# The second expert product of the last two groups as seven block products instead of eight

## The chip, the cores and the metric

The kernel runs on one core of a Trainium2 chip. The metric is the device time of one execution in microseconds (us); lower is better. Before the change the median of three runs is 1410.24 us (1410.23 to 1412.16). One further execution was profiled, and all views below come from it. The engines are named as the profile names them: PE (TensorE, matrix products; PEld is its weight load), DVE (VectorE), ACT (ScalarE), POOL (GpSimd), SP (the engine that issues the DMAs here).

## The reference

An attention over 32 memory slots feeds a mixture of four dense experts that are all computed and weighted:

```
a = softmax(phi, over s)                     # per batch b and head h
k_m, v_m = a^T k, a^T v                      # 32 x 64 each
attn = softmax(q k_m^T / 8)                  # 576 x 32
x = (attn v_m), heads side by side           # 4608 x 512
p = domain_probs / sum(domain_probs)
for e in range(4):
    h = max(x @ w1[e], 0)                    # 4608 x 1024
    out += p[:, e] * (h @ w2[e])             # 4608 x 512
```

Shapes: 8 batches, 8 heads, 576 rows per batch, 512 model columns, 1024 hidden columns, fp32.

## The kernel before

**Numbers.** Every operand of a large product is kept as two fp32r tiles, high part and rest. A product is three matmuls that add up in PSUM: high x high, high x rest, rest x high. The high part is made by an ACT copy (or relu), the rest by a subtraction on DVE or POOL. w1 is multiplied into v_m first (the tiles `vw`), so the first product of an expert is `vw` against the attention weights `AT`.

**Stages.** The rows go in four groups k of two batches (1152 rows, nine tiles of 128). A group takes PAIR = 128 steps: 4 experts x 2 batches (`odd`) x 2 halves of a batch x NJ = 8 blocks j of 128 hidden columns. A batch of 576 rows is cut into 256 + 320 or 320 + 256 rows (`HALF`), so that the 64 rows left over of both batches make the ninth tile (`mid`, name hm).

**One step.** `first(s + 2)` issues six matmuls (lines 553 to 555, two sets of three) of 256 or 320 columns into PSUM, ACT makes relu's high part (line 565), DVE the rest (line 567), into `h` and, for the 64 rows, into `hm`. `second(s)` then multiplies h of two steps ago by w2: three matmuls of 512 columns for each of two row tiles (lines 583 to 585), and three more for hm in the third of four passes. The sum over j stays in PSUM (`p2`, four banks) for eight steps; at the end of a pass `accumulate` lets DVE multiply it by the expert's probability and add it to `acc` in SBUF (lines 603, 605), which goes out after the fourth expert (line 607).

**Other work, by a table of steps.** `plan[s]` holds what is issued ahead of the matmuls of step s. Attention of the later batches stands at the steps of `ATT`. Weights arrive by `take` through four staging tiles (`stage`, line 133) and are split by `split` (ACT line 147, POOL or DVE line 148). For groups 2 and 3 `four` computes the products of w1 and v_m for four batches at once, and writes them to device memory (`vst`, lines 506 to 509, store at 492); `load_vw` (line 531) reads them back. In group 2 this stands in 16 of the 32 steps of each of the first three experts (steps 8 to 23, splits from step 6), one `four` a step. w2 of the next expert is loaded and split at steps 29 to 36 of each expert (`units_w2`), in every group.

**Order.** From step 36 on every engine runs its instructions in the order in which the code issues them (`manual_schedule`); all DMAs are issued by SP, in one queue.

## Time and profile before

| | |
|---|---|
| median of three runs | 1410.24 us |
| profiled execution, span from first to last instruction | 1409.6 us |
| instructions in the span | 21662 |
| first expert of group 2 begins (first matmul of its step 0) | 766.8 us |
| first expert of group 3 begins | 1101.4 us |
| bytes moved by DMA | 200.47 MB, mean 142 GB/s |

The profiled execution gives no time of its own but its span; it is 0.6 us under the median of the runs. In a row of matmuls the time from one start to the next is what PE spends; the duration printed is longer, since matmuls overlap. In a row of a group the columns are: line, engine, operation, tile written and tiles read, shapes, count, then busy us and mean ns of one, then idle time ahead of it and who ended it.

### The profile page before, as it was taken

The page shows a single profiled execution, that of the slowest core. Times are in us where ns is not written, and L with a number is a line of the kernel's source. Part 1 is how long each engine was busy: PE and PEld are TensorE (multiplying, and loading weights), DVE is VectorE, ACT ScalarE, POOL GpSimd, SP SyncE. Part 2 cuts the span into 40 slices and gives each one's busy share as a digit, 9 for nine tenths or more (in the row PEclk, how much of TensorE's full clock was granted, in tenths as well). Part 3 has the DMA queues.
Part 4 walks back from the last instruction along what each step waited for, and adds up shares of the span by engine and source line. Part 5 has one row for each costly group of instructions (what it writes and reads, how often), then busy time and mean ns, then how long its engine had stood idle before and what let it go on. Part 6 is the DMA issues. An engine that isn't in the chain of part 4 may idle for free.

```text
span 1409.6 us, 21662 instructions
## 1 busy us (share of the span) xinstructions
PE 1391.7 (99%) x7742; PEld 1217.9 (86%) x7742; DVE 624.5 (44%) x1470; ACT 579.6 (41%) x1536; POOL 400.7 (28%) x324
## 2 busy tenths in 40 slices
PE   7999999999999999999999999999999999999998
PEld 6888888888888888888888888888888888888887
DVE  7875535435553465344353445434343223222232
ACT  6755555433354456553353434435322312122221
POOL 4400354422234244441342424434220202020200
PEclk9999999999999999999999999999999999999999
DMA  6532332684232243333588675776742623233201
GB/s 251 184 96 75 123 98 91 231 253 128 76 130 95 71 143 109 111 98 105 138 299 243 234 257 173 277 216 224 240 123 64 176 67 105 76 105 76 60 31 38
DMA packets 74363, 200.47 MB, mean 142 GB/s; under 512 B 21904, under 2 KB 23056, under 8 KB 74256
## 3 DMA queue, kind: packets, MB, share of 16 engines
q1 hardware_dynamic: 74256, 199.09, 44.9%
q8 instruction: 62, 1.02, 0.3%
q14 instruction: 45, 0.37, 0.1%
HBM read 146.35 MB, written 51.38 MB: 140 GB/s over the span
## 4 chain that ended last, share of the span: by engine, by line
PE 93%; ACT 2%; DVE 2%; DMA 1%; issue 1%; SPq 0%; ACTq 0%
PE p L585 18%; PE p L583 18%; PE p L584 18%; PE p L553 10%; PE p L554 9%; PE p L555 9%; PE pv L506 3%; PE sc L391 2%; PE x L287 2%; PE pv L461 1%; PE pv L463 1%; PE pv L462 1%; DVE vw L482 1%; DMA stage<-in_w 1%; PE tp L441 1%
## 5 line engine op out<-in xcount | busy, mean ns | idle before, releaser
L148 POOL TENSOR_TENSOR w<-stage,w 128x512 fp32r<-128x512 f32 x230 | 297.2, 1293 | 719.4 <-ACT w L147 698.3
L567 DVE SCALAR_TENSOR_TENSOR h<-p,h 128x256 fp32r<-128x256 f32 x512 | 215.6, 421 | 443.3 <-ACT h L565 300.6
L585 PE MATMUL p<-w,h 128*128 128x512 f32 x1024 | 402.4, 393 | 0.9 <-DVE h L567 0.9
L583 PE MATMUL p<-w,h 128*128 128x512 f32 x1024 | 403.0, 394 | 0.0
L584 PE MATMUL p<-w,h 128*128 128x512 f32 x1024 | 402.3, 393 | 0.0
L565 ACT ACTIVATE h<-p 128x256 fp32r<-128x256 f32 x512 | 196.4, 384 | 484.8 <-PE p L555 465.5
L553 PE MATMUL p<-AT,vw 128*128 128x256 f32 (+1 forms) x1024 | 308.9, 302 | 2.3 <-DVE h L567 0.9
L554 PE MATMUL p<-AT,vw 128*128 128x256 f32 (+1 forms) x1024 | 302.7, 296 | 0.0
L555 PE MATMUL p<-AT,vw 128*128 128x256 f32 (+1 forms) x1024 | 301.5, 295 | 0.0
L585 PEld LDWEIGHTS p<-w,h 128*128 128x128 f32 x1024 | 192.5, 188 | 44.8 <-DVE h L567 1.4
L553 PEld LDWEIGHTS p<-AT,vw 128*128 128x128 f32 x1024 | 193.2, 189 | 22.6 <-DVE h L567 1.2
L583 PEld LDWEIGHTS p<-w,h 128*128 128x128 f32 x1024 | 192.4, 188 | 22.9
L584 PEld LDWEIGHTS p<-w,h 128*128 128x128 f32 x1024 | 192.5, 188 | 21.8
L554 PEld LDWEIGHTS p<-AT,vw 128*128 128x128 f32 x1024 | 193.8, 189 | 19.6
L555 PEld LDWEIGHTS p<-AT,vw 128*128 128x128 f32 x1024 | 192.8, 188 | 0.1
L147 ACT CAST w<-stage 128x512 fp32r<-128x512 f32 x264 | 161.9, 618 | 6.8 <-DMA stage<-in_w 4.6
L567 DVE SCALAR_TENSOR_TENSOR hm<-p,hm 128x64 fp32r<-128x64 f32 x256 | 56.1, 219 | 156.8 <-ACT h L565 155.7
L565 ACT ACTIVATE hm<-p 128x64 fp32r<-128x64 f32 x256 | 57.1, 223 | 161.5 <-PE p L555 161.5
L509 DVE TENSOR_TENSOR vst<-pv,vst 128x512 fp32r<-128x512 f32 x80 | 55.3, 692 | 113.2 <-ACT vst L508 112.9
L276 POOL TENSOR_TENSOR kvs<-stage,kvs 128x512 fp32r<-128x512 f32 x58 | 75.8, 1326 | 103.9 <-ACT kvs L275 103.5
L508 ACT CAST vst<-pv 128x512 fp32r<-128x512 f32 x80 | 46.9, 587 | 123.6 <-PE pv L506 123.6
L482 DVE TENSOR_TENSOR vw<-pv,vw 64x512 fp32r<-64x512 f32 x96 | 65.9, 688 | 24.7 <-ACT vw L480 23.5
(87 smaller groups left out, 1147.4 us busy)
## 6 DMA issues: line engine op xcount, KB each, us to landing
stage<-in_w SPq DMA_DIRECT2D x92, 512.0 KB, 4.2
vwd<-vst SPq DMA_DIRECT2D x80, 512.0 KB, 3.6
vw<-vwd SPq DMA_DIRECT2D x320, 128.0 KB, 3.8
stage<-in_w1d SPq DMA_DIRECT2D x40, 512.0 KB, 3.9
stage<-in_kv SPq DMA_DIRECT2D x32, 512.0 KB, 4.1
stage<-in_qm SPq DMA_DIRECT2D x16, 512.0 KB, 3.9
out<-acc SPq DMA_DIRECT2D x32, 256.0 KB, 2.1
ph<-in_phi SPq DMA_DIRECT2D x16, 288.0 KB, 4.4
```

The source lines that it names most:

```text
L147: nc.scalar.copy(dst[:, 0, :], raw)
L148: eng.tensor_sub(dst[:, 1, :], raw, dst[:, 0, :].bitcast(F32))
L276: eng.tensor_sub(t[:, 1], src, t[:, 0].bitcast(F32))
L482: nc.vector.tensor_sub(t[r, 1, :], ps[r], t[r, 0, :].bitcast(F32))
L553: nc.tensor.matmul(ps, w[:, 0, f], at_t[:, g, 0, c], start=g == 0, stop=False)
L554: nc.tensor.matmul(ps, w[:, 0, f], at_t[:, g, 1, c], start=False, stop=False)
L555: nc.tensor.matmul(ps, w[:, 1, f], at_t[:, g, 0, c], start=False, stop=g == 1)
L565: nc.scalar.activation(t[:, 0, to], ps[:, at_], AF.Relu)
L567: nc.vector.scalar_tensor_tensor(t[:, 1, to], ps[:, at_], 0.0, t[:, 0, to].bitcast(F32), ALU.max, ALU.subtract)
L583: nc.tensor.matmul(po[t], x[:, 0, :], w[:, 0, :], start=j == 0, stop=False)
L584: nc.tensor.matmul(po[t], x[:, 0, :], w[:, 1, :], start=False, stop=False)
L585: nc.tensor.matmul(po[t], x[:, 1, :], w[:, 0, :], start=False, stop=j == NJ - 1)
```

## The change

For groups 2 and 3 (`SEVEN = 2`), `first` and `second` are replaced by 64 units. A unit is 256 rows (two tiles of 128) against 512 hidden columns (four blocks j) and all 512 columns of w2: the work of four steps. It is a 2 x 2 block product (row tiles x halves of the hidden columns, times halves of the hidden columns x halves of the output columns). It is computed from seven block products in place of eight, by Winograd's form of Strassen's scheme: the left sides are A11, A12, A22 and four sums t1, t2, t3, n4 of blocks, the right sides blocks of w2 and four sums of them. Each product is six matmuls of 256 columns. The first product of the experts (`rows`, now lines 854 to 856) and the 64 left-over rows (`middle`) are computed as before.

- Left sums are made by DVE straight from PSUM with the relu (`x_out`, `y_diff`, `y_last`), then split by ACT and POOL.
- Products add up in two PSUM banks in turn; some partial sums are added to `acc` for one output block, and then the next product is accumulated on top. So DVE adds seven times 256 columns per unit (`add_in`) in place of two times 512 columns per eight steps.
- The sums of w2 (`sums`, eight jobs in groups 0 and 1 by the table `JOBS`) are made by POOL, split, and kept in device memory, as is the split w2 of group 1 (`leave`, `leave_now`). `units_w2` is gone for groups 2 and 3: a block of four units reads eight tiles of 512 KB back into a ring of eleven (`load_part`, `free`).
- PSUM is one tile of eight banks with turns kept by hand. In the units banks 2 to 5 hold the first product and 6 and 7 the seven products; two banks are left for the other work.
- The reading back of `vw` for groups 2 and 3 stands at other steps (`VW_LOAD_7`), and so do the last transposes of batch 7.

```diff
-    7: (PAIR + 62, PAIR + 88, (2 * PAIR + 98, 2 * PAIR + 102, 2 * PAIR + 106), (2 * PAIR + 112, 2 * PAIR + 113, 2 * PAIR + 114)),
+    7: (PAIR + 62, PAIR + 88, (2 * PAIR + 98, 2 * PAIR + 102, 2 * PAIR + 106), (2 * PAIR + 115, 2 * PAIR + 116, 2 * PAIR + 117)),
...
+SEVEN = 2
+BEGIN = SEVEN * PAIR
+UNITS = (NG - SEVEN) * E * 2 * 4
+Q = 256
+X_BANK, Y_BANK, AB_BANK = 4, 2, 6
+JOBS = (92, 101, 110, 119, 127, PAIR + 23, PAIR + 62, PAIR + 86)
+VW_LOAD_7 = ((18, 32), (24, 40))
+FIRST_LOADS = (PAIR + 112, PAIR + 121, PAIR + 122, PAIR + 123, PAIR + 124, PAIR + 125, PAIR + 126, PAIR + 127)
 
...
-    psum = pool("psum", space=PSUM)
+    banks = pool("psum", space=PSUM).tile([P, 8, 512], F32, name="banks")
+    turns = {"pm": [0, 0, 4], "p2": [0, 4, 4]}
...
+        if k == SEVEN - 1:
+            leave(("w2", e, j), t)
...
+    def leave_now():
+        for key, t in leaving:
+            kept_for[key] = dram.tile([P, 2, DM], F32, name="k" + "".join(map(str, key)))
+            nc.sync.dma_start(kept_for[key], t.bitcast(F32))
+        leaving.clear()
+    def sums(s, e, fh):
+        kept = []
+        top, low = slice(0, Q), slice(Q, DM)
+        sub, g = nc.gpsimd.tensor_sub, nc.gpsimd
+        at(s, (("w2", e, 2 * fh), kept.append))
+        at(s + 1, (("w2", e, 2 * fh + 1), kept.append))
+        at(s + 1, lambda: g.tensor_add(kept[1][:, :, low], kept[0][:, :, low], kept[1][:, :, low]))
+        at(s + 2, lambda: sub(kept[0][:, :, low], kept[0][:, :, top], kept[0][:, :, low]))
+        at(s + 2, lambda: sub(kept[0][:, :, top], kept[1][:, :, low], kept[0][:, :, top]))
+        at(s + 3, lambda: sub(kept[1][:, :, top], kept[1][:, :, top], kept[0][:, :, top]))
+        def out(i):
+            t = att.tile([P, 2, DM], F32R, name="sv", tag="kvs", bufs=KVS)
+            split(t, kept[i // 2][:, i % 2, :], g)
+            leave(("v", e, fh, i), t)
+        for i in range(4):
+            at(s + 3 + i, lambda i=i: out(i))
+            at(s + 4 + i, leave_now)
...
-        if s >= LAST:
+        if s >= BEGIN:
...
-            for j2 in range(4):
+            for j2 in range(4 if nk < SEVEN else 0):
                 for i, u in enumerate(units_w2(nk, ne, j2)):
                     at(s + W2_FROM + 2 * j2 + i, u)
+                    if nk == SEVEN - 1:
+                        at(s + W2_FROM + 2 * j2 + i + 1, leave_now)
...
-                    at(s + VW_LOAD_AT[odd][fh], lambda a=(nk, ne, odd, fh): load_vw(*a))
+                    when = VW_LOAD_AT if nk < SEVEN else VW_LOAD_7
+                    at(s + when[odd][fh], lambda a=(nk, ne, odd, fh): load_vw(*a))
...
+    for n, s in enumerate(JOBS):
+        sums(s, n // 2, n % 2)
+    for s in FIRST_LOADS:
+        at(s, lambda: load_part(wp.tile([P, 2, DM], F32R, name="w2", tag="w2", bufs=NJ + 1)))
...
+    def free(u, *which):
+        if u % 4 == 3:
+            for i in which:
+                ring.extend(W[u // 4][i, jj] for jj in range(2))
...
+    def open_ring():
+        ring.append(wp.tile([P, 2, DM], F32R, name="w2", tag="w2", bufs=NJ + 1))
+        ring.append(att.tile([P, 2, 512], F32R, name="vw", tag="vw1", bufs=5))
+        ring.append(wp.tile([P, 2, 512], F32R, name="w1", tag="w1", bufs=4))
...
+    def x_out(u):
+        if u >= UNITS:
+            return
+        g = ph2["g"]
+        a = work.tile([P, 2, 2, P], F32R, name="a1", tag="h", bufs=AHEAD + 2)
+        t = work.tile([P, 2, 2, P], F32R, name="t1", tag="h", bufs=AHEAD + 2)
+        VE.scalar_tensor_tensor(g[:, 2], ps_of(u, 0)[:, 1], 0.0, g[:, 0], ALU.max, ALU.subtract)
+        AC.copy(a[:, 0], g[:, 0])
+        GP.tensor_sub(a[:, 1], g[:, 0], a[:, 0].bitcast(F32))
+        mids(u, 0)
+        AC.copy(t[:, 0], g[:, 2])
+        GP.tensor_sub(t[:, 1], g[:, 2], t[:, 0].bitcast(F32))
+        op["a11", u], op["t1", u] = a, t
+    def y_hi(u):
+        if u < UNITS:
+            AC.activation(ph2["Y"][u % 2][:, 0], flat_of(u, 1), AF.Relu)
+    def y_diff(u):
+        if u < UNITS:
+            src, g, d = ps_of(u, 1)[:, 1], ph2["g"], ph2["d"]
+            for i in range(2):
+                VE.scalar_tensor_tensor(d[:, i], src, 0.0, g[:, 1 + i], ALU.max, ALU.subtract)
+    def y_lo(u):
+        if u >= UNITS:
+            return
+        y, d, D = ph2["Y"][u % 2], ph2["d"], ph2["D"][u % 2]
+        VE.scalar_tensor_tensor(y[:, 1], flat_of(u, 1), 0.0, y[:, 0].bitcast(F32), ALU.max, ALU.subtract)
+        op["a12", u], op["a22", u] = y[:, :, :, :P], y[:, :, :, P:]
+        AC.copy(D[:, 0], d)
+        GP.tensor_sub(D[:, 1], d, D[:, 0].bitcast(F32))
+        op["t3", u], op["t2", u] = D[:, :, 0], D[:, :, 1]
+    def y_last(u):
+        if u >= UNITS:
+            return
+        n, N4 = ph2["n"], ph2["N"][u % 2]
+        VE.scalar_tensor_tensor(n, ps_of(u, 1)[:, 0], 0.0, ph2["d"][:, 1], ALU.max, ALU.subtract)
+        mids(u, 1)
+        AC.copy(N4[:, 0], n)
+        GP.tensor_sub(N4[:, 1], n, N4[:, 0].bitcast(F32))
+        op["n4", u] = N4
...
+    def product(u, name, place, side, b, start, stop):
+        a, ps = op[name, u], banks[:, AB_BANK + (u + b) % 2, :Q]
+        c = slice(Q * side, Q * side + Q)
+        for jj in range(2):
+            w = W[u // 4][place, jj]
+            for i, (l, r) in enumerate(((0, 0), (0, 1), (1, 0))):
+                nc.tensor.matmul(
+                    ps, a[:, l, jj], w[:, r, c],
+                    start=start and jj + i == 0, stop=jj == 1 and i == 2, skip_group_check=True,
+                )
+    def add_in(u, b, tile_i, side, first):
+        k, e, fh, odd, half = place_of(u)
+        t0 = (0, 2, 5, 7)[2 * odd + half]
+        if e == 0 and fh == 0 and (k, t0) not in acc:
+            a = work.tile([P, 1024], F32, name="acc", tag="acc", bufs=4)
+            for i in range(2):
+                acc[k, t0 + i] = a[:, i * DM:i * DM + DM]
+        n = TP * k + t0 + tile_i
+        a, p = acc[k, t0 + tile_i][:, Q * side:Q * side + Q], pt[:, n, e:e + 1]
+        src = banks[:, AB_BANK + (u + b) % 2, :Q]
+        if first and e == 0 and fh == 0:
+            VE.tensor_scalar_mul(a, src, p)
+        else:
+            VE.scalar_tensor_tensor(a, src, p, a, ALU.mult, ALU.add)
...
+    def middle(u, part):
+        k, e, fh, odd, half = place_of(u)
+        if (odd, half) != (1, 0):
+            return
+        if part == 0:
+            held["m"] = bank("pm", DM)
+        ps = held["m"]
+        for i in (2 * part, 2 * part + 1):
+            x, w = hm[:, 4 * fh + i], W[u // 4][part, i % 2]
+            nc.tensor.matmul(ps, x[:, 0], w[:, 0], start=i == 0, stop=False)
+            nc.tensor.matmul(ps, x[:, 0], w[:, 1], start=False, stop=False)
+            nc.tensor.matmul(ps, x[:, 1], w[:, 0], start=False, stop=i == 3)
...
+    def unit(u):
+        s = BEGIN + 4 * u
+        run_plan(s)
+        product(u, "a11", 0, 0, 0, True, False)
+        rows(u + 1, 1, 0)
+        add_in(u, 0, 0, 0, True)
+        run_plan(s + 1)
+        middle(u, 0)
+        product(u, "a12", 1, 0, 1, True, True)
+        rows(u + 1, 1, 1)
+        add_in(u, 1, 0, 0, False)
+        y_hi(u + 1)
+        product(u, "t2", 2, 0, 0, False, False)
+        free(u, 0)
+        load_parts()
+        y_diff(u + 1)
+        add_in(u, 0, 0, 1, True)
+        run_plan(s + 2)
+        y_lo(u + 1)
+        middle(u, 1)
+        product(u, "t3", 2, 1, 1, True, False)
+        free(u, 2)
+        y_last(u + 1)
+        rows(u + 2, 0, 0)
+        add_in(u, 1, 1, 1, True)
+        product(u, "t1", 3, 1, 0, False, False)
+        run_plan(s + 3)
+        load_parts()
+        add_in(u, 0, 1, 1, False)
+        product(u, "n4", 1, 1, 1, False, True)
+        free(u, 1)
+        rows(u + 2, 0, 1)
+        add_in(u, 1, 0, 1, False)
+        x_relu(u + 2)
+        product(u, "a22", 3, 0, 0, False, True)
+        free(u, 3)
+        load_parts()
+        send(u, 0)
+        x_out(u + 2)
+        add_in(u, 0, 1, 0, True)
+        send(u, 1)
...
-        steps(FREE, LAST)
+        steps(FREE, BEGIN - 3)
+        open_seven()
+        steps(BEGIN - 3, BEGIN - 2)
+        for jj in range(2):
+            rows(0, 0, jj)
+        x_relu(0)
+        x_out(0)
+        steps(BEGIN - 2, BEGIN - 1)
+        turns["pm"] = [0, 0, 2]
+        for jj in range(2):
+            rows(0, 1, jj)
+        y_hi(0)
+        y_diff(0)
+        y_lo(0)
+        y_last(0)
+        steps(BEGIN - 1, BEGIN)
+        for jj in range(2):
+            rows(1, 0, jj)
+        x_relu(1)
+        x_out(1)
         accumulate()
+        open_ring()
+        for u in range(UNITS):
+            unit(u)
```

**PE, group 3, a plain place.** The names: p is a PSUM tile, w a split weight, AT the attention weights. Before, one step:

```order
L553 MATMUL p_14177<-AT,vw 128x256
L554 MATMUL p_14177<-AT,vw 128x256
L555 MATMUL p_14177<-AT,vw 128x256
L553 MATMUL p_14177<-AT,vw 128x256
L554 MATMUL p_14177<-AT,vw 128x256
L555 MATMUL p_14177<-AT,vw 128x256
L583 MATMUL p_14153<-w_13628,h 128x512
L584 MATMUL p_14153<-w_13628,h 128x512
L585 MATMUL p_14153<-w_13628,h 128x512
L583 MATMUL p_14157<-w_13628,h 128x512
L584 MATMUL p_14157<-w_13628,h 128x512
L585 MATMUL p_14157<-w_13628,h 128x512
```

Now, in the middle of a unit: the products with t2 and t3 (their left sides lie in what was vt), the first product of the unit after next, the product with t1:

```order
L940 MATMUL banks<-w_7872,vt_83 128x256 x3
L940 MATMUL banks<-w_7909,vt_83 128x256 x3
L940 MATMUL banks<-w_7872,vt_83 128x256 x3
L940 MATMUL banks<-w_7909,vt_83 128x256 x3
L854 MATMUL banks<-AT,vw 128x320
L855 MATMUL banks<-AT,vw 128x320
L856 MATMUL banks<-AT,vw 128x320
L854 MATMUL banks<-AT,vw 128x320
L855 MATMUL banks<-AT,vw 128x320
L856 MATMUL banks<-AT,vw 128x320
L940 MATMUL banks<-vw,t_14580 128x256 x3
L940 MATMUL banks<-w_7974,t_14580 128x256 x3
```

The 512-column matmuls are gone, and a weight load stands before every 256 or 320 columns.

**DVE, group 2, second expert, where `four` runs.** Before, four steps: the subtraction of `four`, then the rests of hm and h.

```order
L509 TENSOR_TENSOR vst<-pv,vst 128x512
L567 SCALAR_TENSOR_TENSOR hm<-p_9614,hm 128x64
L567 SCALAR_TENSOR_TENSOR h<-p_9614,h 128x256
L509 TENSOR_TENSOR vst<-pv,vst 128x512
L567 SCALAR_TENSOR_TENSOR hm<-p_9649,hm 128x64
L567 SCALAR_TENSOR_TENSOR h<-p_9649,h 128x256
L509 TENSOR_TENSOR vst<-pv,vst 128x512
L567 SCALAR_TENSOR_TENSOR hm<-p_9683,hm 128x64
L567 SCALAR_TENSOR_TENSOR h<-p_9683,h 128x256
L509 TENSOR_TENSOR vst<-pv,vst 128x512
L567 SCALAR_TENSOR_TENSOR hm<-p_9715,hm 128x64
L567 SCALAR_TENSOR_TENSOR h<-p_9715,h 128x256
```

Now one unit, the same stretch of work (L958 is `add_in`, L912 `y_diff`, L918 `y_lo`, L928 `y_last`, L896 `x_out`, L990 the left-over rows' addition):

```order
L544 TENSOR_TENSOR vst<-banks,vst 128x512
L958 SCALAR_TENSOR_TENSOR acc<-banks,pt,acc 128x256
L912 SCALAR_TENSOR_TENSOR ph<-banks,ph 128x256 x2
L958 SCALAR_TENSOR_TENSOR acc<-banks,pt,acc 128x256
L544 TENSOR_TENSOR vst<-banks,vst 128x512
L918 SCALAR_TENSOR_TENSOR a<-banks,a 128x512
L990 SCALAR_TENSOR_TENSOR accm<-banks,pt,accm 128x512
L928 SCALAR_TENSOR_TENSOR xs<-banks,ph 128x256
L958 SCALAR_TENSOR_TENSOR acc<-banks,pt,acc 128x256
L544 TENSOR_TENSOR vst<-banks,vst 128x512
L958 SCALAR_TENSOR_TENSOR acc<-banks,pt,acc 128x256 x2
L896 SCALAR_TENSOR_TENSOR ph<-banks,ph 128x256
```

The subtractions of `four` now stand between additions, for each of which a product on PE waits.

149 lines of the change are left out of this document (137 added, 12 removed).

## The prediction

> **What bounds the kernel now.** I read the busy times and the chain of waits first, and then the stages.
>
> ```profile
> PE 1391.7 (99%) x7742; PEld 1217.9 (86%) x7742; DVE 624.5 (44%) x1470; ACT 579.6 (41%) x1536; POOL 400.7 (28%) x324
> PE 93%; ACT 2%; DVE 2%; DMA 1%; issue 1%; SPq 0%; ACTq 0%
> ```
>
> PE is never idle and carries 93% of the chain that ended last, so only PE's own time is worth anything. The next view gives the stretches of the four experts of group 2, of the first of group 3, and three short ones. Its columns are busy time of PE, weight load, DVE, ACT and POOL, granted clock, DMA share and GB/s.
>
> ```profile
> 766.80:853.50 86.70, 86.70 (x478) 76.08 (x477) 36.65 (x81) 35.32 (x90) 31.07 (x25) 1.00 0.73 239
> 853.50:937.80 84.30, 84.30 (x455) 72.99 (x454) 39.00 (x86) 36.05 (x93) 31.05 (x25) 1.00 0.71 231
> 937.80:1020.50 82.70, 82.70 (x442) 72.09 (x441) 32.45 (x73) 34.46 (x88) 31.06 (x25) 1.00 0.71 229
> 1020.50:1101.40 80.90, 80.90 (x459) 70.95 (x458) 30.70 (x78) 20.65 (x62) 10.24 (x9) 1.00 0.39 108
> 1101.40:1176.70 75.30, 75.30 (x410) 66.03 (x409) 21.63 (x57) 18.20 (x56) 10.33 (x9) 1.00 0.36 100
> 740.00:745.00 5.00, 5.00 (x26) 4.29 (x25) 1.62 (x5) 1.58 (x5) 1.88 (x2) 1.00 0.97 244
> 755.00:760.00 5.00, 5.00 (x29) 4.33 (x28) 1.33 (x4) 1.15 (x3) 0.00 (x0) 1.00 1.06 344
> 810.00:830.00 20.00, 20.00 (x102) 17.29 (x101) 8.62 (x20) 9.02 (x24) 7.97 (x7) 1.00 0.86 290
> ```
>
> The clock is full everywhere. Group 3 is products alone. The first three experts of group 2 are another stage: DMA is busy over 0.7 of the time, and DVE, ACT and POOL about 40%.
>
> **What a matmul costs.** The instructions in order of time, one step of 256 rows and one of 320:
>
> ```profile
> 1101.43 0.28 PE L553 MATMUL p<-AT,vw 128*128 128x256 f32 x1
> ...
> 1102.14 0.40 PE L583 MATMUL p<-w,h 128*128 128x512 f32 x1
> ...
> 1103.52 0.28 PE L553 MATMUL p<-AT,vw 128*128 128x256 f32 x1
> ```
> ```profile
> 700.38 0.40 PE L583 MATMUL p<-w,h 128*128 128x512 f32 x1
> ...
> 701.77 0.31 PE L553 MATMUL p<-AT,vw 128*128 128x320 f32 x1
> ...
> 702.65 0.40 PE L583 MATMUL p<-w,h 128*128 128x512 f32 x1
> ```
>
> Six matmuls of 256 columns take 0.71 us, 0.118 each; six of 320 take 0.88, 0.147 each; six of 512 take 1.38 to 1.39, 0.231 each. An expert is 16 steps of 2.09, 16 of 2.27 and 24 left-over matmuls (5.5): 75.3, which is the stretch 1101.40 to 1176.70. So PE stalls nowhere there.
>
> **1. The columns saved.** A unit had 24 matmuls of 512 in its second product (5.54); now it has 42 of 256 (42 x 0.118 = 4.96). That is 0.58 less, 4.7 for the eight units of an expert, and **-37.5** for eight experts. The rest of PE's work stays.
>
> This takes each 256-column matmul with its own weight load at 0.118 in long runs too. The chain of waits shows one such run:
>
> ```profile
> 150.09 0.95 PE x L287 x8
> 151.04 0.12 PE x L290
> ...
> 151.86 0.23 PE p L583
> ```
>
> From 150.09 to 151.86 stand fifteen in a row (eight, one, and six of the first product): 1.77, again 0.118. A load prints longer than that, but loads overlap:
>
> ```profile
> 902.10 0.19 PEld L554 LDWEIGHTS p<-AT,vw 128*128 128x128 f32 x1
> 902.24 0.31 PE L554 MATMUL p<-AT,vw 128*128 128x320 f32 x1
> 902.25 0.19 PEld L555 LDWEIGHTS p<-AT,vw 128*128 128x128 f32 x1
> ```
>
> The load that begins at 902.10 is over at 902.29, after its matmul and the next load began. The Trainium skill speaks against the change here: "TensorE: Matmul & The Clock Gate", its part 3 on packing small matmuls, says that a weight load overlaps a running matmul only where it fills another row group; and these all fill the whole array. With its figure for a load, 128 / 1.2 = 107 ns, the 18 loads more per unit would add 1.9 us, and the sum would be some 120 us slower. The trace contradicts it.
>
> **2. The hand-over in a plain unit.** Two PSUM banks take seven products, so a product waits until DVE has read the one before it in its bank. The tightest place is from t2 to n4. The durations:
>
> ```profile
> 1162.63 0.42 DVE L567 SCALAR_TENSOR_TENSOR h<-p,h 128x256 fp32r<-128x256 f32 x1 [2.36 <-ACT h L565]
> 1162.97 1.40 DVE L603 TENSOR_SCALAR acc<-p,pt 128x512 f32<-128x512 f32 x2
> ```
> ```profile
> L605 DVE SCALAR_TENSOR_TENSOR acc<-p,pt,acc 128x512 f32<-128x512 f32 x96 | 67.2, 742 | 2.6 <-PE p L585 2.6
> L509 DVE TENSOR_TENSOR vst<-pv,vst 128x512 fp32r<-128x512 f32 x80 | 55.3, 692 | 113.2 <-ACT vst L508 112.9
> L565 ACT ACTIVATE h<-p 128x256 fp32r<-128x256 f32 x512 | 196.4, 384 | 484.8 <-PE p L555 465.5
> L147 ACT CAST w<-stage 128x512 fp32r<-128x512 f32 x264 | 161.9, 618 | 6.8 <-DMA stage<-in_w 4.6
> L508 ACT CAST vst<-pv 128x512 fp32r<-128x512 f32 x80 | 46.9, 587 | 123.6 <-PE pv L506 123.6
> L148 POOL TENSOR_TENSOR w<-stage,w 128x512 fp32r<-128x512 f32 x230 | 297.2, 1293 | 719.4 <-ACT w L147 698.3
> ```
>
> A DVE operation of 256 elements takes 0.42, and the next may start 0.34 after it. An addition of 256 to `acc` isn't in the trace; it lies between 0.34 and the 0.74 of 512, and I take 0.39 to the next start, by the nearer row. A matmul of 256 ends 0.16 after the next one's start (0.28 less 0.118), and DVE starts 0.03 after that, as the last rows show (1404.25 + 0.39, then 1404.67):
>
> ```profile
> 1404.25 0.39 PE L585 MATMUL p<-w,h 128*128 128x512 f32 x1
> ...
> 1404.67 1.43 DVE L605 SCALAR_TENSOR_TENSOR acc<-p,pt,acc 128x512 f32<-128x512 f32 x2 [2.58 <-PE p L585]
> ...
> 1404.93 0.39 PE L585 MATMUL p<-w,h 128*128 128x512 f32 x1
> ```
>
> With t2's start as zero, DVE does y_diff from 0.19 to 0.87, t2's addition from 0.90, y_lo (512) from 1.29, y_last from 1.90, the left-over rows' rest (0.13, in half of the units), and t3's addition from 2.24 or 2.37, over at 2.7 to 2.85. PE reaches n4 after four sets of 0.71, at 2.83, or at 3.0 where the first product has 320 columns. So it nearly fits: a stall of about 0.1 in one unit in four. I put **+2** for the 52 units without `four`; the ends are 0, and 0.3 in each (an addition at 0.5, a wake-up 0.1 later), 16.
>
> **3. The hand-over where `four` runs.** Twelve units of group 2 hold four `four`s each, and each adds two matmuls (0.46) on PE, a cast (0.62) and a copy (0.59) on ACT, and a subtraction (0.61 to the next start) on DVE. One stands between t2's addition and y_lo. Its matmuls end at 1.33, ACT's copy at 1.95 or, with a cast ahead, 2.57; DVE's subtraction ends 0.6 later, and y_lo, y_last and t3's addition follow (0.61 + 0.34 + 0.45): 4.0 to 4.6. PE, with its own two `four`s, is at n4 at 3.75. The next `four` stands ahead of t1's addition, for which a22 waits in the same way. By these sums a unit loses 0.25 to 0.9 at n4 and 0.4 to 1.0 at a22. The later operations shift along, so I take 0.9 in all, **+11**; ends 0 and 12 x 1.9 = 23. POOL's subtractions (four of 1.29 for `four`, and five halves of it for the unit) make 8.4 of a unit's 10.7 us, so POOL is covered, but not by much.
>
> **4. DMA in the first three experts of group 2.** They moved 20.7, 19.5 and 18.9 MB (rate by length), 59.1 in all. The raw w2 goes (3 x 2.1), and 16 tiles of 0.524 MB per expert come: 78 MB. The stretch at 1.06 ran at 344 GB/s and the one at 0.86 at 290: 325 to 337 at full share, so 78 MB need 236 us. PE needs 253.7 - 14 + 11 = 250. That is 94% of the queue's capacity, with 3 MB of it asked for in the last unit of each block of four, on top of the stores of `four`:
>
> ```profile
> vwd<-vst SPq DMA_DIRECT2D x80, 512.0 KB, 3.6
> stage<-in_w1d SPq DMA_DIRECT2D x40, 512.0 KB, 3.9
> ```
>
> Loads are asked for 7 to 9 us before they are used, against 4 us to land; a queue 5 us long eats that. I take **+5**, some 1.5 per expert; the ends are 0 and the rival below. The Trainium skill ("DMA: Bandwidth & Descriptors", the table of measured bandwidth) gives 425 GB/s for 16 MB read by a core whose neighbour is idle; by that 78 MB would take an estimated 184 us, this term would fall to nothing, and the sum would be 5 lower. The trace differs: its share is at 1 with 344 GB/s.
>
> **5. The rest.** DVE's softmax for batches 6 and 7 falls into units.
>
> ```profile
> L417 DVE TENSOR_REDUCE z<-at 128x16 f32<-128x512 f32 x16 | 10.8, 675 | 0.5 <-ACT at L410 0.5
> L420 DVE TENSOR_TENSOR at<-at,z 128x512 f32<-128x512 f32 x16 | 11.8, 736 | 0.4
> ```
>
> These two alone are 1.4 in front of an addition that has 1.0 of slack, and two small ones come between: 0.4 to 1.0 per score tile, six tiles, **+4** (0 to 8). The eight jobs of w2 sums add 8 x 8 POOL operations of 1.29 and 64 stores of 0.5 MB to groups 0 and 1, where POOL and the queue have gaps; SP is held up behind them, and a late staging tile costs PE a microsecond here and there: **+2** (0 to 10). At the end one addition of 256 stands in place of two of 512: **-0.4**.
>
> Sum: -37.5 + 2 + 11 + 5 + 4 + 2 - 0.4 = -13.9 against the span of 1409.6. The median of the runs lies 0.6 above the span, so I add that: **1396 us**.
>
> **Rivals.** *All covers hold*: DVE's additions are shorter than I took, ACT copies early, and only terms 1 and 5's end remain: 1410.2 - 37.9 = 1372. For it speaks that DVE is busy about 70% in the worst unit; against it, that its order is fixed and each wait is in series.
>
> *DMA bounds group 2* (the slower side). Its place is the first three experts; it decides once their mix of reads and stores moves under 78 MB / 269 us = 290 GB/s, since then the 19 us over PE's 250 take the rest of the gain. The stretch at 740 had the queue 0.97 busy at only 244 GB/s; the one at 810 didn't pass 290. At 270 GB/s it costs 289 - 250 = 39, in place of 5: 1430. At 244 it is 320 - 250 = 70: 1461.
>
> *The preparation stalls groups 0 and 1*: the sums hold two of four staging tiles for six steps (13 us); if each job makes PE wait 1.5 us, term 5 is 12, not 2: 1406, no change to speak of.
>
> *The change saves no columns on PE*, because loads don't hide: at the printed 0.188 a load, 18 x 64 x 0.188 = 217 more, over 1580. The run of fifteen excludes it almost wholly.
>
> **How the numbers follow.** My forecast, 1384 to 1407, has a chance of 0.5. All covers hold, 1371 to 1384: 0.19. Preparation stalls, or terms 2 to 4 together near their upper ends, 1407 to 1413: 0.11. DMA bounds group 2, above 1413: 0.19. Loads don't hide: 0.01. The range leaves out about 0.07 below 1375 and 0.12 above 1425. A measurement of this kernel can tell 0.2%, about 3 us, from no change. Faster than 1407.4: 0.7; within: 0.08; slower: 0.22.
>
> **What would show it.** Right: the experts of group 3 take 70.6 to 71 us and not 75.3, a unit of 256 rows 7.8. In group 2's first three experts waits of PE's products for DVE's additions (n4, a22) stand at about 1 us per unit. Wrong: waits for w2 parts ahead of products, with DMA share at 1 (the DMA rival); a wait of n4 in every unit of group 3 (term 2's upper end); 256-column matmuls further than 0.118 apart (loads); or group 2 beginning later than 766.8 by more than 3 us (preparation).

## The result, and the profile after

The changed kernel takes **1538.7 us** (median of four runs, 1538.6 to 1541.6), against 1410.6 of the kernel before on the same chip: ratio 1.0911, 95% interval 1.0896 to 1.0927. The forecast was 1396, with 1375 to 1425 as its range. The page of the profile after begins:

```profile
span 1536.7 us, 25126 instructions
...
PE 1407.2 (92%) x8894; PEld 1267.6 (82%) x8894; DVE 805.8 (52%) x1862; ACT 657.6 (43%) x1568; POOL 617.3 (40%) x580
...
DMA packets 99724, 292.97 MB, mean 191 GB/s; under 512 B 24720, under 2 KB 25872, under 8 KB 99600
```

92.5 MB more are moved than before, and PE, which had hardly a gap, is 129.5 us short of the span. Where the 127.1 us between the two spans lie (an expert's or a unit's time is taken from the start of a matmul of its first product to the same place in the next):

| | before | after |
|---|---|---|
| step 252 (end of group 1), later than before by | | 71.9 |
| first unit of group 2 begins | 766.8 | 849.0 |
| group 2's experts | 86.7, 84.3, 82.7, 80.9 | 102.7, 96.8, 93.8, 81.4 |
| group 3's experts | 75.3 each | 78.2 each |

The two starts in the second row are not quite the same place: the units run their first products further ahead, so some 7 us of the 82.2 between them come back at the end of the kernel; the 71.9 of the row above compares like with like. So the loss falls in all three places, and more than half of it ahead of the first unit. Windows of 100 us show it; the columns are the window, its length, the busy time of each engine, the granted clock, the share of the DMA engines and GB/s. In the kernel before the same windows have PE at 100.00 and the clock at 1.00.

```profile
400.00:500.00 100.00, 86.63 (x460) 74.70 (x459) 36.36 (x86) 46.06 (x114) 51.16 (x42) 0.95 0.58 206
...
900.00:1000.00 100.00, 86.14 (x617) 80.30 (x616) 61.66 (x139) 43.18 (x91) 46.55 (x47) 0.95 0.78 254
```

The sums of waits by engine (who waits at which line for whom: us in all, times, the longest) name the suspects:

```profile
ACT sv L148 <- DMA kv<-sv: 45.6, 7, 11.3
ACT vst L543 <- DMA vwd<-vst: 37.1, 13, 8.8
```
```profile
PE banks L940 <- DVE acc L958: 49.6, 43, 7.3
PE banks L618 <- ACT h L600: 19.6, 4, 7.2
PE banks L496 <- DVE vw L517: 14.5, 5, 5.9
```

ACT waits for a buffer of a w2 sum (`sv`, tag kvs) and of `four` (`vst`, the same tag) until a store has landed; PE waits for ACT and, in the units, for DVE's additions. The last is PE at L496 (the first matmul of w1 with v_m in groups 0 and 1); the same matmul of the kernel before (L461) is not among PE's waits.

A plain unit of group 3, from t2's first matmul on (start, duration, instruction, in brackets the idle time ahead and who ended it):

```profile
1305.58 1.58 PE L940 MATMUL banks<-w,vt 128*128 128x256 f32 x12
1305.78 0.60 ACT L906 ACTIVATE a<-banks 128x512 fp32r<-128x512 f32 x1 [2.43 <-PE banks L856]
1306.49 0.76 DVE L912 SCALAR_TENSOR_TENSOR ph<-banks,ph 128x256 f32<-128x256 f32 x2 [1.09 <-ACT a L906]
...
1308.15 0.42 DVE L928 SCALAR_TENSOR_TENSOR xs<-banks,ph 128x256 f32<-128x256 f32 x1
1308.60 0.28 ACT L868 ACTIVATE hm<-banks 128x128 fp32r<-128x128 f32 x1 [0.70 <-DVE xs L928]
...
1309.12 1.07 DVE L958 SCALAR_TENSOR_TENSOR acc<-banks,pt,acc 128x256 f32<-128x256 f32 x2
1309.65 0.98 PE L940 MATMUL banks<-w,tl 128*128 128x256 f32 x6 [0.89 <-DVE acc L958]
```

The columns behave as forecast: twelve matmuls of 256 in a row take 1.58 with the last one's end, 0.118 from start to start. But DVE's y_diff (L912) begins 0.91 after t2's start and not 0.19. It reads nothing that y_hi (L906) writes; both read the same PSUM banks, and DVE begins 0.11 after ACT has ended (1305.78 + 0.60 = 1306.38). The same happens in turn for the left-over rows: ACT's read (L868) waits for DVE's y_last (L928), and DVE's (L869) for ACT. So t3's addition, the first of the two at 1309.12, comes 3.54 after t2's start, and n4 (L940, tl) waits 0.89. The Trainium skill ("PSUM — Partial Sum Buffer", the section on bank collisions) says that two engines must not read one bank at a time and that compilers order such reads; these rows agree, and term 2 had left it out.

### The profile page after: what moved, and what is told of

Same layout as the page of the kernel before. It is cut to its first block, busy times and chain, and to the rows that moved or that the text cites. A ratio compares the mean times of both kernels' runs of the same rounds, so it can differ in the third digit from the quotient of the medians.

```text
span 1536.7 us, 25126 instructions
## 1 busy us (share of the span) xinstructions
PE 1407.2 (92%) x8894; PEld 1267.6 (82%) x8894; DVE 805.8 (52%) x1862; ACT 657.6 (43%) x1568; POOL 617.3 (40%) x580
## 4 chain that ended last, share of the span: by engine, by line
PE 67%; DVE 11%; DMA 8%; ACT 6%; issue 4%; POOL 3%; SPq 1%; DVEq 0%; ACTq 0%; POOLq 0%
PE banks L940 14%; PE banks L618 7%; PE banks L619 7%; PE banks L620 7%; PE banks L588 4%; PE banks L589 4%; PE banks L590 4%; DMA vwd<-vst 4%; PE banks L856 3%; PE banks L854 3%; PE banks L855 3%; DMA kv<-sv 2%; DVE ph L912 2%; PE banks L426 2%; PE banks L322 2%
## 5 line engine op out<-in xcount | busy, mean ns | idle before, releaser
L958 DVE SCALAR_TENSOR_TENSOR acc<-banks,pt,acc 128x256 f32<-128x256 f32 x416 | 194.7, 479 | 93.0 <-PE banks L940 88.9
L602 DVE SCALAR_TENSOR_TENSOR h<-banks,h 128x256 fp32r<-128x256 f32 x256 | 107.4, 421 | 243.2 <-ACT h L600 177.6
L618 PE MATMUL banks<-w,h 128*128 128x512 f32 x512 | 205.8, 402 | 19.9 <-ACT h L600 19.6
L619 PE MATMUL banks<-w,h 128*128 128x512 f32 x512 | 204.6, 400 | 0.0
L620 PE MATMUL banks<-w,h 128*128 128x512 f32 x512 | 203.9, 398 | 0.0
L600 ACT ACTIVATE h<-banks 128x256 fp32r<-128x256 f32 x256 | 97.7, 384 | 198.5 <-PE banks L590 169.9
L588 PE MATMUL banks<-AT,vw 128*128 128x256 f32 (+1 forms) x512 | 158.6, 310 | 13.1 <-DVE vw L517 6.7
L921 POOL TENSOR_TENSOR vt<-ph,vt 128x512 fp32r<-128x512 f32 x64 | 82.9, 1296 | 202.2 <-ACT vt L920 202.2
L940 PE MATMUL banks<-w,a 128*128 128x256 f32 x1080 | 157.1, 287 | 6.8 <-DVE acc L640 2.7
L940 PEld LDWEIGHTS banks<-w,a 128*128 128x128 f32 x1080 | 143.5, 191 | 17.2 <-issue 7.0
L589 PE MATMUL banks<-AT,vw 128*128 128x256 f32 (+1 forms) x512 | 152.7, 298 | 0.0
L854 PE MATMUL banks<-AT,vw 128*128 128x256 f32 (+1 forms) x512 | 152.7, 298 | 0.0
L855 PE MATMUL banks<-AT,vw 128*128 128x256 f32 (+1 forms) x512 | 152.3, 298 | 0.0
L590 PE MATMUL banks<-AT,vw 128*128 128x256 f32 (+1 forms) x512 | 152.2, 298 | 0.0
L856 PE MATMUL banks<-AT,vw 128*128 128x256 f32 (+1 forms) x512 | 152.2, 297 | 0.0
L618 PEld LDWEIGHTS banks<-w,h 128*128 128x128 f32 x512 | 98.5, 192 | 33.3 <-ACT h L600 21.5
L588 PEld LDWEIGHTS banks<-AT,vw 128*128 128x128 f32 x512 | 97.8, 191 | 27.4 <-DVE vw L517 9.9
L620 PEld LDWEIGHTS banks<-w,h 128*128 128x128 f32 x512 | 98.1, 192 | 23.3 <-DVE h L602 1.0
L940 PE MATMUL banks<-w,tl 128*128 128x256 f32 x384 | 62.9, 300 | 51.4 <-DVE acc L958 46.9
```

Source lines behind the costliest of these rows:

```text
L588: nc.tensor.matmul(ps, w[:, 0, f], at_t[:, g, 0, c], start=g == 0, stop=False)
L589: nc.tensor.matmul(ps, w[:, 0, f], at_t[:, g, 1, c], start=False, stop=False)
L590: nc.tensor.matmul(ps, w[:, 1, f], at_t[:, g, 0, c], start=False, stop=g == 1)
L618: nc.tensor.matmul(po[t], x[:, 0, :], w[:, 0, :], start=j == 0, stop=False)
L619: nc.tensor.matmul(po[t], x[:, 0, :], w[:, 1, :], start=False, stop=False)
L620: nc.tensor.matmul(po[t], x[:, 1, :], w[:, 0, :], start=False, stop=j == NJ - 1)
```

## The experiments

Where no interval stands, the time is that of one run; the kernel before took 1410.6 to 1411.6 beside it.

### Groups 0 and 1

**1. The preparation alone**, put into the kernel before.

```diff
+    for n, s in enumerate(JOBS):
+        sums(s, n // 2, n % 2)
```

> The kernel before, with the preparation alone added (the eight jobs of w2 sums on POOL at the same steps, their splits, and the stores of sums and of group 1's split w2); nothing reads what is stored, and groups 2 and 3 are computed as before. If the 82 us that group 2 begins late come from the preparation, group 2 begins 70 to 80 us later than 766.8 here too, and the total is 1480 to 1492. If they come from something else in the changed kernel (the tile of eight banks, a lower clock of that program, code size), group 2 begins within 15 us of 766.8 and the total is under 1425.

Measured: 1470.9, and from step 240 on every step is 60.0 later than before. That is less than the 70 to 80 expected (part of the 82 was the different starting place), but far from the rival's 15. So the preparation makes 60 of the 72; 12 are something else. The longest stop and its aftermath:

```profile
447.23 1.31 SPq L181 DMA_DIRECT2D kv<-sv  x1
454.23 0.62 ACT L151 CAST sv<-stage 128x512 fp32r<-128x512 f32 x1 [7.65 <-DMA kv<-sv]
...
455.18 0.80 PE L621 MATMUL p<-w,h 128*128 128x512 f32 x1 [7.64 <-ACT h L603]
```
```profile
447.50:455.00 7.50, 0.04 (x1) 0.73 0.99 371
...
459.50:461.00 1.50, 1.50 (x6) 0.50 1.04 421
461.00:462.50 1.50, 1.50 (x9) 0.92 0.58 238
```

A store of a sum issued at 447.23 has landed by 454.2; ACT has waited 7.65 for its buffer, the relu behind it is late, and PE stands 7.64. In all, ACT waits 47.4 us for these buffers, at eight places. The last rows (window, length, PE busy, granted clock, DMA share, GB/s) show what comes on top: after the stop PE runs at half its clock for some 6 us, which costs 3 more. The steps around it lose 10.7 in all.

**2. Who waits for the buffer**: the sums' high part is copied by POOL in the changed kernel.

```diff
-            split(t, kept[i // 2][:, i % 2, :], g)
+            raw = kept[i // 2][:, i % 2, :]
+            g.tensor_copy(t[:, 0, :], raw)
+            g.tensor_sub(t[:, 1, :], raw, t[:, 0, :].bitcast(F32))
```

> The changed kernel, with the high part of each w2 sum copied by POOL and not by ACT, so that only POOL waits for the buffers (kvs) whose stores land late. If ACT's wait for those buffers is what stops PE in groups 0 and 1, most of the 82 us go: group 2 begins less than 25 us later than 766.8, total 1470 to 1485. If it is the stores themselves or SP's queue that hold the staging loads (or POOL's extra work), group 2 still begins 60 or more late, total 1515 or more.

Measured: 1539.3, with group 2 only 1.5 us less late than in the changed kernel: the rival's figures, and the theory in this form fell. The wait itself only moved, and the loads behind POOL now reach ACT late (21.5 us for w's staging tiles, against 8.6):

```profile
POOL sv L196 <- DMA kv<-sv: 40.5, 7, 11.1
```
```profile
ACT w L148 <- DMA stage<-in_w: 21.5, 7, 9.9
```

**5 and 6. Sums that are not stored, and copies alone**, both in the kernel before.

```diff
-            leave(("v", e, fh, i), t)
```

> The kernel before with the preparation alone, as in the first experiment (1470.9, group 2 begins 60 late), but the w2 sums are made and split and not stored (32 stores of 512 KB less; the copies of the split w2 are still stored). If the stops come from the three kvs buffers, which come free only when a store has landed, group 2 begins less than 25 us late and the total is under 1435. If it is the work of POOL and ACT, or the staging tiles that the sums hold for six steps, group 2 still begins 45 or more late, total over 1455.

```diff
-    for n, s in enumerate(JOBS):
-        sums(s, n // 2, n % 2)
```

> The kernel before with only the 32 stores of group 1's split w2, and no w2 sums at all. If the sums make the stops, group 2 begins less than 8 us late and the total is 1411 to 1419. If the bytes written, or SP's queue with 32 stores more, make them, it is 1430 or more.

Measured: 1432.9 and 1412.3. Both came out as the first reading had it. Of the 60 us some 38 hang on the stores of the sums: the first experiment's waits put them at the three buffers that come free only when a store has landed. Some 21 hang on the sums' own work (POOL, ACT, staging tiles held for six steps; these three were not separated, but the fifth's longest stop, 5.1, is a wait for a staging load). The 32 copies make 1.3, though they move the same 16.8 MB as the sums' stores, so these bytes alone are not it.

**7 and 8. Group 3 alone, and the turn of the banks.**

```diff
-SEVEN = 2
+SEVEN = 3
-JOBS = (92, 101, 110, 119, 127, PAIR + 23, PAIR + 62, PAIR + 86)
+JOBS = (213, 247, 310, 343, 357, 364, 371, 378)
```

> Seven products in group 3 alone (group 2 as before the change), the additions' order of the third experiment, and the eight jobs of w2 sums at steps of few staging loads (213, 247, 310, 343, 357, 364, 371, 378), none in group 0. If the cost of a job is set by what else asks for staging and kvs buffers at its steps, group 3 begins less than 12 us later than 1101.4, its experts take 71 each, and the total is 1396 to 1408, less than before. If a job costs its 7 us wherever it stands, group 3 begins 50 or more late and the total is 1445 or more.

Measured: 1438.1, between the two forecasts. Group 3's experts take 71.1 each, but it begins 40 late. Behind step 212 some 25 of these are lost (20 in the eighth), so a job costs about 3, neither next to nothing nor 7. The other 14.9 us are lost ahead of step 212, where no job has run (the copies make 1.3 of them). What stands there is a product that waits for a bank (first the seventh kernel, then the eighth at the same place):

```profile
596.87 0.50 PE L496 MATMUL banks<-w,vt 128*128 128x512 f32 x1 [1.58 <-DVE vw L517]
```
```profile
586.05 0.39 PE L509 MATMUL banks<-w,vt 128*128 128x512 f32 x1
```

The changed kernel gives out the four banks in a fixed turn (`turns`). In the kernel before, the pool did not: its banks come in orders such as 2310, then 2301. The eighth puts that order in as a table (and the last transposes of batch 7 back to their old steps, behind the places compared here).

```diff
-        out = banks[:, base + n % size, :]
+        at = int(TURNS[n]) if size == 4 and base == 0 and n < len(TURNS) else n % size
+        out = banks[:, base + at, :]
```

> The seventh experiment's kernel (1438.1), with one thing changed: up to the first unit the four PSUM banks of the tag pm are given out in the order in which they stood in the kernel before (a table of bank numbers), and not in a fixed turn 0, 1, 2, 3; the last transposes of batch 7 stand at their old steps. In the seventh experiment step 212, ahead of all jobs, began 14.7 us later than before, and only 1 to 2 of it are the copies' stores. If the fixed turn of banks makes this (a product waits for a bank that is still read while another is free), step 212 begins less than 4 us late and the total is 1422 to 1427. If the single tile of eight banks does it through other waits, or the program's size, nothing changes: 1436 to 1440.

Measured: 1424.5, 13.6 less; the wait at that place is gone. Step 212 is 5.5 late and not under 4, all of it lost near step 164, where the copies also cost the sixth experiment 2.2; there the clock halved behind a stop of 2.0 us in the eighth and not in the sixth (the last section has why). 60.0 and 13.6 are 73.6, against the 71.9 of groups 0 and 1. The two were measured in different kernels, one run each, so the sum is a sign that little is missing and no more.

### The plain unit

**3. Another order in the units.**

```diff
-        y_diff(u + 1)
         add_in(u, 0, 0, 1, True)
+        y_diff(u + 1)
...
-        y_lo(u + 1)
-        y_last(u + 1)
         rows(u + 2, 0, 0)
         add_in(u, 1, 1, 1, True)
+        y_lo(u + 1)
+        y_last(u + 1)
```

(and ACT's read of the left-over rows moved to right behind the relu, `mids_hi`).

> The changed kernel, with another order in the units only: ACT reads the left-over rows' high part right behind the unit's relu, DVE does t2's addition ahead of y_diff (which must wait for ACT's read of the same bank), and t3's addition ahead of y_lo and y_last. If the order and the taking of turns of ACT and DVE at a bank make the loss in the plain units, group 3's experts fall from 78.2 to 71 to 73 us and the total by 20 to 40. If DVE's amount of work or its durations make it, group 3's experts stay within 1 us of 78.2.

Measured: 1501.1, and group 3's experts take 71.1 to 71.2. The same place as above:

```profile
1288.72 1.58 PE L951 MATMUL banks<-w,vt 128*128 128x256 f32 x12
...
1289.62 0.48 DVE L969 SCALAR_TENSOR_TENSOR acc<-banks,pt,acc 128x256 f32<-128x256 f32 x1 [1.10 <-PE banks L951]
...
1290.69 0.48 DVE L969 SCALAR_TENSOR_TENSOR acc<-banks,pt,acc 128x256 f32<-128x256 f32 x1
...
1291.73 0.88 PE L951 MATMUL banks<-w,tl 128*128 128x256 f32 x6
```

t3's addition (the second L969) now begins 1.97 after t2's start, not 3.54, and n4 follows its predecessor without a wait.

**11. Half of that edit**: only `mids_hi`, DVE's additions as in the changed kernel.

> The changed kernel (group 3's experts 78.2, units 9.99, 9.84, 10.59, 8.69) with only half of the third experiment's edit: ACT reads the left-over rows right behind the unit's relu, so that the turn ACT, DVE, ACT, DVE at a bank becomes ACT, ACT, DVE, DVE; DVE's additions stay where they are. If the extra turn at the bank makes most of the plain units' loss, the units whose successor has left-over rows (the first two of four) fall by 0.7 or more each and the expert to 74 to 76. If the order of DVE's additions makes it, the experts stay at 77.5 to 78.5.

Measured: 1523.5, the experts 76.0, the first two units of four 9.43 and 9.27, not 9.99 and 9.84. The turn ACT, DVE, ACT, DVE at a bank makes 2.2 of the 7.1 us of an expert; the other 4.9 go with the order of DVE's additions (t2's ahead of y_diff, t3's ahead of y_lo and y_last; which of the two does more was not tried). Both readings hold in part, and the first one's 0.7 per unit was a little too large.

### Group 2

**4. Without most reads of w2 parts.**

```diff
+        for block in range(1, UNITS // 4):
+            W[block] = W[0]
```

> The changed kernel, with the w2 parts read back for the first block of four units alone; all later blocks use those (so expert, half and group get the wrong parts). The time is that of the kernel without 120 of its 128 reads of 512 KB. If these reads hold back the stores of four in SP's queue, the three stops of 7 us (at 903, 1006 and 1100) go, and group 2's first three experts are 8 to 12 us shorter each (102.7, 96.8, 93.8 in the changed kernel). If the stops come from ACT and DVE in four itself, those experts stay within 3 us.

This kernel leaves out 120 of the 128 reads and multiplies with the first block's parts throughout, so it gives a time and not the reference's result. Measured: 1513.0; group 2's experts 93.1, 86.5, 85.8, 81.4. The stops of 7 us are gone: 27.9 in all. In the changed kernel the first of them looks like this:

```profile
895.53 0.32 SPq L527 DMA_DIRECT2D vwd<-vst  x1
...
899.35 10.89 SPq L566 DMA_DIRECT2D vw<-vwd  x8
907.13 0.59 ACT L543 CAST vst<-banks 128x512 fp32r<-128x512 f32 x1 [8.35 <-DMA vwd<-vst]
910.45 1.65 PE L940 MATMUL banks<-w,tl 128*128 128x256 f32 x6 [7.34 <-DVE acc L958]
```

The store of `four` issued at 895.53, behind six reads of parts issued from 890.20 on, lands at 907.05, 11.5 us later, and only then has ACT its buffer. This reads as if reads stood ahead of stores in SP's queue. Leaving reads out takes away their bytes too, so:

**13. All bytes, but the stores of `four` issued by ACT.**

```diff
-            nc.sync.dma_start(vwd[key], t.bitcast(F32))
+            nc.scalar.dma_start(vwd[key], t.bitcast(F32))
```

> The changed kernel (1538.7; group 2's first three experts 102.7, 96.8 and 93.8) with all its bytes and reads, but with the stores of four (vwd) issued by ACT, so that they no longer stand in SP's queue behind the reads of w2 parts and of vw. If the place in SP's queue makes the three stops of 7 us, they go as they did without the reads (93.1, 86.5, 85.8): the three experts fall by 5 to 10 each and the total to 1508 to 1523. If the bytes make them (the DMA rival), the experts stay within 3 us and the total is 1532 or more.

Measured: 1541.9; 104.3, 97.0, 94.5. The first stop of 7.3 became two of 4.0 and 1.4, other waits grew, and nothing was gained: the place in SP's queue alone is not it. Windows of the changed kernel, and then of the fourth experiment's (last three columns: granted clock, DMA share, GB/s):

```profile
885.00:890.00 5.00, 5.00 (x40) 4.83 (x39) 3.79 (x9) 3.35 (x7) 2.96 (x3) 1.00 0.95 278
...
895.00:900.00 5.00, 5.00 (x37) 4.82 (x37) 3.49 (x8) 2.50 (x5) 3.19 (x3) 1.00 1.03 418
900.00:905.00 5.00, 2.35 (x15) 1.70 (x13) 0.04 (x1) 0.00 (x0) 0.00 (x0) 0.91 1.02 414
```
```profile
895.00:900.00 5.00, 5.00 (x36) 4.82 (x37) 3.38 (x8) 3.62 (x9) 4.13 (x5) 1.00 0.82 290
900.00:905.00 5.00, 4.41 (x32) 3.89 (x31) 3.88 (x10) 3.78 (x8) 3.52 (x4) 1.00 1.03 257
```

In the changed kernel the DMA engines are nearly full (0.87 to 1.06) for some 25 us, because the parts of a block are asked for together, in the last unit of the block ahead, when their tiles come free. A store of `four` issued into that burst lands late; its buffer stops ACT, and ACT stops PE. The mean over 50 us is 0.75 to 0.82, which is why an average had not shown it.

The landing times of the 80 stores of `four` help to tell the two causes apart. In the changed kernel the two issued ahead of each of the three stops take 10.2 to 12.7 us; issued by ACT none takes more than 8.6; without the reads none takes more than 7.2, and the median is 3.6. So the place in SP's queue is worth 3 to 4 us of a store's landing, and the bytes of the burst, the forecast's own rival in another form, make most of the rest. The thirteenth gained nothing from that, since in it ACT itself waits for earlier DMAs ahead of its stores. The Trainium skill ("DMA: Bandwidth & Descriptors", on issuing engines) says that DMAs of different issuers share the same engines and that a second issuer saves little; this run's total agrees, though the stores of the burst landed sooner. Reads that are spread out, which would show what the burst costs, weren't tried.

### A version that is faster

Group 3 alone needs eight jobs whose cost is below its gain. **9** starts from the eighth: sums stored by ACT, splits two steps apart, later jobs.

```diff
+            (nc.scalar if key[0] == "v" else nc.sync).dma_start(kept_for[key], t.bitcast(F32))
...
+JOBS = (341, 357, 369, 381, 393, 407, 421, 435)
```

> The eighth experiment's kernel, with the stores of the w2 sums issued by ACT and not by SP, the four splits of a job two steps apart, and the jobs at steps 341, 357, 369, 381 and, inside group 3, 393, 407, 421 and 435. If the jobs' cost is the wait of kvs buffers for stores that stand in SP's queue behind loads, the eight jobs cost less than 8 us in all and the total is 1396 to 1408, below the kernel before. If it is the work of ACT and POOL or the bytes, the jobs still cost 20 or more: 1416 or more.

Measured: 1436.8, not the 1396 to 1408 of the expectation. Parts were read late, behind a staging load that waited for a tile held by a job:

```profile
1133.45 0.33 SPq L147 DMA_DIRECT2D stage<-in_w  x1
1133.88 0.86 SPq L802 DMA_DIRECT2D w<-kv  x2
```
```profile
1140.49 0.98 PE L964 MATMUL banks<-w,t 128*128 128x256 f32 x3 [8.07 <-DMA w<-kv]
```

**10** has other steps, and asks for a job's loads only when a tile is free.

```diff
+        ahead = 2 if order[i][0] == "sum" else STAGE
+        stage_ahead(i + ahead if i >= len(early) else i + 1)
```

> The ninth experiment's kernel (1436.8, of which 8.5 fell at step 352 and some 25 in the first two experts of group 3, behind staging loads that stood in SP's queue for a tile that a job still held), with the jobs at steps 363, 375, 388, 400, 412, 424, 436 and 448, and with loads for the sums that are not asked for ahead of a free tile. If SP's queue made those losses, group 3 starts less than 6 us late, its units lose less than 5 us in all against 71.1 per expert, and the total is 1398 to 1406, faster than before. If ACT's and POOL's work for the jobs makes them, units with jobs take 2 to 3 us more and the total is 1415 to 1430.

Measured: 1442.0, ratio 1.0222 (1.0205 to 1.0239), outside both forecasts. Group 3 began in time; now the loads were too late, and POOL, with the unit's own work behind it, waited for them:

```profile
1293.48 0.35 SPq L147 DMA_DIRECT2D stage<-in_w  x1
1297.98 1.26 POOL L202 TENSOR_TENSOR stage<-stage 128x512 f32<-128x512 f32 x1 [14.40 <-DMA stage<-in_w]
1304.50 1.62 PE L965 MATMUL banks<-w,a 128*128 128x256 f32 x6 [12.79 <-DVE acc L983]
```

**12** has `ahead = 3`.

> The tenth experiment's kernel (1442.0), where the five longest stops of group 3 (3.8 at 1136, 7.0 at 1169, 3.7 at 1259, 12.8 at 1292 and 2.3 at 1113) follow POOL's wait for a staging tile of a job whose load was issued too late, behind loads of vw. One number changes: the loads for the sums are asked for one job ahead (three loads, not two). If the late loads make the stops, units 2, 5, 14 and 17 of group 3 fall from 17.1, 17.1, 16.9 and 23.4 to under 11.5 each, and the total is 1399 to 1407, faster than before. If POOL's work for the jobs in the units makes them, they stay over 13 and the total is 1425 or more.

Measured: 1414.5, ratio 1.0012 (1.0000 to 1.0023). The units named fell to 10.6, 8.2, 10.6 and 8.2, as forecast, but the total did not reach 1407; one new stop of 3.9 stood at 1230, at a read that fell among a job's DMAs.

**14** moves the jobs to 363, 373, 385, 401, 417, 433, 449 and 465.

> The twelfth experiment's kernel (1414.5; group 3's experts 74.3, 77.8, 72.4 against 71.1), with the jobs at steps 363, 373, 385, 401, 417, 433, 449 and 465, so that none runs in the last unit of a block of four, when the next block's parts are read. If the remaining loss is a read of a part that falls together with a job's stores and loads (the stop of 3.9 at 1230, and 2.3 at the first unit), the three experts come to 71 to 73 and the total is 1399 to 1407. If it is POOL's and ACT's work for the jobs, the loss moves with them and the total stays at 1411 to 1418.

Measured: 1423.5, ratio 1.0087 (1.0073 to 1.0101). The stop at the read went, and six of 2.3 came, one per job. The loss moved with the jobs, as the rival had it, but it grew, past the rival's 1418, and neither text had the mechanism:

```profile
1133.70 1.30 POOL L163 TENSOR_TENSOR sv<-stage,sv 128x512 fp32r<-128x512 f32 x1
1135.03 0.33 ACTq L192 DMA_DIRECT2D kv<-sv  x1
1135.40 0.60 ACT L930 ACTIVATE a<-banks 128x512 fp32r<-128x512 f32 x1 [3.65 <-PE banks L965]
...
1136.94 0.47 DVE L981 TENSOR_SCALAR acc<-banks,pt 128x256 f32<-128x256 f32 x1
1137.47 0.98 PE L965 MATMUL banks<-w,tl 128*128 128x256 f32 x6 [2.20 <-DVE acc L981]
```

The store issued by ACT waits until POOL's rest ends at 1135.00, y_hi (L930) stands behind it on ACT, y_diff and t3's addition behind that, and n4.

**15 and 16** put the jobs at 363, 375, 384, 400, 416, 432, 448 and 464, so that, by the order in the code, the store stands at the unit's start and not ahead of y_hi; the sixteenth issues the copies by ACT too.

> The twelfth experiment's kernel (1414.5, ratio 1.0012), with the jobs 2 to 7 at steps 384, 400, 416, 432, 448 and 464: each begins at the first step of a unit (as in the twelfth, where five of six such jobs cost under 2 us; one step later, in the fourteenth, each cost 2.3 and its aftermath) and ends before the last unit of its block of four, in which the next parts are read (the stop of 3.9 at 1230). If a job's cost is set by where its POOL instructions fall in a unit and its stores among the reads, group 3's experts come to 71.1 to 73.5 and the total is 1402 to 1409. If a job costs its 2 us wherever it stands, the total stays at 1411 to 1418.

> The fifteenth experiment's kernel, with the copies of the split w2 in groups 0 and 1 issued by ACT too. In the kernels with the copies in group 1, 2 to 5 us were lost near step 164, where attention of batch 5 asks for its keys behind those stores in SP's queue. If their place in SP's queue makes this, step 352 begins 2 to 5 us earlier than in the fifteenth and the total falls by as much. If the bytes make it, or ACT now waits for its own stores, the total is the same or larger.

Measured: **1404.2**, ratio to the kernel before 0.9941 (0.9929 to 0.9954), and 1403.1, ratio 0.9940 (0.9926 to 0.9953). So seven products in group 3 alone save 7 us, 0.6%, clear of the noise. Group 3's first three experts take 71.7, 71.1 and 71.1. The sixteenth changes nothing that can be told: in its profile the loss near step 164 is 4.7, and 2.5 in the fifteenth's, where the clock stayed whole. A window of the fifteenth in which two whole jobs run, and parts of two more:

```profile
1200.00:1300.00 100.00, 100.00 (x778) 98.23 (x778) 61.55 (x151) 40.85 (x87) 64.56 (x67) 1.00 0.84 273
```

PE has no gap, and POOL is at 65%.

## Why the prediction was wrong, step by step

- **Term 1, columns, -37.5: right.** 256-column matmuls stand 0.118 apart with their loads, and with the third experiment's order an expert of group 3 takes 71.1, where 70.6 to 71 was forecast (70.6 without any wait).
- **Term 2, the plain unit, +2 (0 to 16): wrong, about +57.** The step that failed is "DVE does y_diff from 0.19 to 0.87": it waits until ACT's read of the bank has ended and begins at 0.91. That moves y_last from 1.90 to 2.57; the left-over rows' turn at the bank adds another 0.5, and t3's addition begins at 3.54 and not at 2.24 or 2.37, past the 2.83 to 3.0 at which PE is at n4. The sum took the order of instructions on each engine, and left out that two engines take turns at a bank. The loss is 7.1 per expert (78.2 less 71.1), times eight; that it is as large in group 2 is assumed. The kernel before had shown it:

```profile
906.71 0.23 ACT L565 ACTIVATE hm<-p 128x64 fp32r<-128x64 f32 x1
...
907.24 0.22 DVE L567 SCALAR_TENSOR_TENSOR hm<-p,hm 128x64 fp32r<-128x64 f32 x1 [0.22 <-ACT h L565]
```

  The rest of hm began at 907.24, when ACT's read for h had ended, though its own high part was ready at 906.94 and DVE was free from 907.02.
- **Term 3, `four`, +11: too large.** Without the reads, the third expert of group 2 is 7.6 above one of group 3, and 16 times PE's own 0.46 is 7.4. So about +1 is left for three experts, on top of the 7.1 that group 3's 78.2 holds already; what `four` would cost in a unit that does not wait was not measured.
- **Term 4, DMA in group 2, +5: the mechanism was the rival's, mis-sized.** The stops cost 27.9. The forecast compared an expert's bytes with its time (94% of capacity); what counts is the 25 us at a share near 1, and what waits is not a product for its part but ACT for a buffer whose store has not landed. The rival's point of 290 GB/s did not decide: the burst reached 418.
- **Term 5.** Softmax, +4 (0 to 8): about 0. Without the reads the last two units of group 2's first expert are 5.2 above the same two of its second, and its fourth expert is 3.2 above group 3's; but PE's own matmuls for the attention of batches 6 and 7 make 4.0 and 5.6 in these places in the kernel before (steps 24 to 31 take 22.7 and 18.7; the fourth expert 80.9 and group 3's 75.3), and they are no loss of the change. Preparation, "+2 (0 to 10)": **wrong, 60.** It priced SP's and POOL's work by their average gaps and missed that a job's fourth split needs a buffer whose store has to land first, and that ACT and POOL wait for it in order. "Group 2 beginning later than 766.8 by more than 3 us" was named as its sign and came true. The fixed turn of the banks, 13.6, was in no term, though the diff shows it.

-37.5 + 57 + 1 + 28 + 0 + 60 + 13.6 = 122, against 127.1 measured; the 0.5 per expert by which 71.1 is above 70.6 makes 4 more. That the sum comes so close is in part luck: the rows come from different kernels, and they overlap. The third experiment gave back 37.6 of the 57, since group 2's units, with 8.1 of their 28 (4 times 7.1), still met the DMA stops.

## What to carry to other kernels

Price a preparation by what its buffers wait for, from the request to the landing of a store, and not by the work of the engines that make it: here work that fitted into POOL's gaps cost PE 60 us. A store or load stands in an order on the engine that issues it; moving it helps only where nothing urgent is behind it (the ninth, tenth and fourteenth experiments each moved the wait to another queue). And where several edits come in one change, the places that look neutral, here a bank's turn, deserve a row of their own.
